# The expert's VectorE and ScalarE work put behind attention's own in each step, and weights four steps later

## The chip, the cores and the metric

The kernel runs on one core of a Trainium2 chip. The metric is the device time of one execution in microseconds, the median of several runs. [...] Each engine works through its own queue in the order in which it was given.

## The reference

Attention with a causal mask over 2 batches, 12 heads, 448 positions and a head width of 64; then two feed-forward layers over the 896 x 768 result.

```python
# attention, per batch and head
scores = scale * q @ k.T ; scores masked above the diagonal
attn   = exp(scores - max) / (sum + 1e-9)
x      = (attn @ v), heads side by side        # 896 x 768
# first layer (w_in 768 x 2048, w_out 2048 x 768)
h = x @ w_in ; g = h - tanh(h) ; x = g @ w_out
# second layer (w_a, w_b 768 x 1536, w_out 1536 x 768)
out = ((x @ w_a) * (x @ w_b)) @ w_out
```

All is in float32; the weights arrive as float64, read as pairs of 32-bit words.

## The kernel before, in words

**Precision.** A product is made of three TensorE matmuls: each operand is split into a high part of reduced precision and a low part, and `matmuls` (L189 to 196) adds high x high, high x low and low x high. So every weight tile needs preparation, and so does every activation.

**Weights.** A weight tile (768 x 128 for `w_in`) goes through five stages. `load_part` (L105) issues half of it as a transfer on SP. `magnitude` (L119) takes the absolute value of the high word on ScalarE (L125). `bits_step` (L134) does four VectorE operations, one at a call (L142, L144, L148, L152), that turn the two words of a float64 into one float32; the last one frees the raw buffer, of which there are two. `split` (L159) rounds to the high part `wh` on ScalarE (L166) and subtracts to get the low part `wl`, on POOL during attention (L168).

**Attention.** Heads go in pairs: 12 pairs `i`, each with 4 row blocks `c` of 112 queries, give 48 units. The loop in `attention` takes steps j = 0 to 51. Step j issues, in this order for every engine: the scores of unit j (L263, into two `s` banks); the transposes of unit j - 2's weights (`turn_p`, L307, into `t` banks, with every third turn in the `h` bank for the first 24 units); in steps with c = 1 and c = 2 the products with the values of the pair before (L328), and in c = 2 the transposes of the reciprocal sums (`turn_r`, L345); then on ScalarE and VectorE what was put off. `later_act` holds ScalarE's copies out of the `t` banks (L318, L354); it runs first. Then `top` (L275, VectorE, the masked minimum, which also moves the scores out of their bank) and `exps` (L287, ScalarE). Then `later_dve`: VectorE's copies (L316) and `divide` (L357, with POOL's L358 and L359, which split the result). In steps with c = 0 there follow the reciprocal of the sums (L337, VectorE, which waits for POOL's L401), its widening (L339) and the split of the next pair's `q` and `k` (L250, L251), both on POOL.

**Expert work inside attention.** `filler` is called three times a step. Its third call feeds the weights: loads in steps 3, 6, 9 and 12, and from step `WEIGHTS_AT` on one `bits` call a step, a `magnitude` where j % 4 is 0, a `split` where it is 1, and loads from step 24 on. From step 28 on the first two calls issue three and two matmuls of the first layer for the first batch. `early` makes five such tiles of 128 hidden units, each of 18 matmuls into the one `h` bank. A tile takes four steps, and the next one starts two steps after the last one's end: tiles begin in steps 28, 33, 38, 43 and 48 and end in steps 31, 36, 41, 46 and 51. A tile needs its weights split two steps earlier. `hidden` (L428) then queues the tile's element work: `tanh` (L441, ScalarE), `rest` (L437, VectorE: h - tanh, the last reader of the `h` bank), and in the step after that `gh` (L438, ScalarE) and `gl` (L439, VectorE). In the kernel before, these go into the same two queues as attention's work: `tanh` ahead of the step's `exps`, `rest` behind the step's copies and ahead of `divide`.

**Who sets the order.** Attention is written inside `manual_schedule`, so the order of its instructions on each engine is the written one. What follows, the other batch's part of the tiles and both layers, is ordered by a planner; it may put such instructions between attention's. Its matmuls go to `s`, `h`, `t` and `o` banks in a cycle, and a bank of a name is given out in the written order.

Of the kernel before, what the change touches and what calls it, by code (L numbers as in the profile page):

```python
# [48 lines left out]
def attention_moe_moe2(ctx, tc, q, k, v, w_in, w_out, w_a, w_b, w_o, out):  # L49
    nc = tc.nc  # L50
    B, H, S, D = v.shape
# [1 line left out]
    DFF1 = w_in.shape[1]  # L53
    DFF2 = w_a.shape[1]
    XLAG = 7
    WEIGHTS_AT = 16
    GROUP_P = (2, 4, 3, 4)
    QC = 112
    NQ = S // QC
# [17 lines left out]
    def bank(tag):  # L77
        return ps.tile([128, 512], F32, tag=tag, name=tag, bufs=BANKS[tag])
# [50 lines left out]
    def bits(steps):  # L129

        for _ in range(steps):
            bits_step()
# [68 lines left out]


    later_act, later_dve, turn_no = [], [], [0]
    in_attention = [True]
    xh, xl = {}, {}

    def attention(filler):
        with ExitStack() as st:
# [45 lines left out]
            def scores(j):  # L254

                i, c = units[j]
                n = (c + 1) * QC
                cs = slice(c * QC, n)
                sc[j] = [bank("s")[:QC, :n], bank("s")[:QC, :n]]
                for x, (a, b_) in enumerate(parts[i]):  # L260
                    for e in range(2):
                        r = slice(64 * e, 64 * e + 64)
                        nc.tensor.matmul(  # L263
                            sc[j][e], a[r, 0, cs], b_[r, 1, :n], start=x == 0, stop=x == len(parts[i]) - 1
                        )
# [32 lines left out]
            def turn_p(j):  # L298

                i, c = units[j]  # L300
                p = pr.pop(j).rearrange("q h (k s) -> q (h k) s", s=QC)
                nb = 2 * (c + 1)
                for a in range(0, nb, GROUP_P[c]):
                    g = GROUP_P[c]
                    pst = turn_bank(j)
                    for x in range(g):
                        nc.tensor.transpose(  # L307
                            out=pst[:QC, x * QC:(x + 1) * QC], in_=p[:, a + x], identity=ident[:QC, :QC]
                        )
                    out_ = pts[c // 2][:, :, :c + 1, c % 2]  # L310
                    if g == nb:
                        in_ = pst[:QC, :g * QC].rearrange("s (e k q) -> s e k q", e=2, q=QC)
                    else:
                        out_, in_ = out_[:, a // g], pst[:QC, :g * QC].rearrange("s (k q) -> s k q", q=QC)
                    if c in (0, 2) or (c == 3 and a):
                        later_dve.append(lambda o=out_, p=in_: nc.vector.tensor_copy(out=o, in_=p))  # L316
                    else:
                        later_act.append(lambda o=out_, p=in_: nc.scalar.copy(out=o, in_=p))  # L318

            def values(i, h):  # L320

                vt, o = vs[i % NV], bank("o") if h == 0 else ot[i]
                ot[i] = o
                for k_ in range(2 * h + 2):
                    c0 = max(2 * h, k_)
                    cs = slice(c0 * QC, (2 * h + 2) * QC)
                    for e in range(2):
                        nc.tensor.matmul(  # L328
                            o[64 * e:64 * e + 64, cs], vt[:, k_, e, :],
                            pts[h][:, e, k_, c0 - 2 * h:].rearrange("s c q -> s (c q)"),  # L330
                            start=k_ == 0, stop=k_ == 2 * h + 1, skip_group_check=True,
                        )
# [9 lines left out]
            def turn_r(i):  # L342
                r, pst, o = sums.pop(i), turn_bank(NQ * i), ot[i]
                for c in range(NQ):
                    nc.tensor.transpose(  # L345
                        out=pst[:, c * QC:(c + 1) * QC], in_=r[:, c].rearrange("q h d -> q (h d)"),
                        identity=ident[:QC, :QC],
                    )
                b, kk = pairs[i]
                if kk not in xh:  # L350
                    xh[kk], xl[kk] = [xp.tile([128, NT], F32R, tag=x, name=x) for x in ("xh", "xl")]
                hi, lo = [t[kk][:, b * S:(b + 1) * S] for t in (xh, xl)]
                x, y = [sp.tile([128, S], F32, tag=t, name=t, bufs=2) for t in "xy"]
                later_act.append(lambda: nc.scalar.copy(out=y, in_=pst[:, :S]))  # L354

                def divide():
                    nc.vector.tensor_tensor(out=x, in0=o[:, :S], in1=y, op=ALU.mult)  # L357
                    nc.gpsimd.tensor_copy(out=hi, in_=x)  # L358
                    nc.gpsimd.tensor_tensor(out=lo, in0=x, in1=hi.bitcast(F32), op=ALU.subtract)  # L359

                divides.append(lambda: later_dve.append(divide))

            def run(queue):
                todo, queue[:] = queue[:], []
                for f in todo:
                    f()
# [5 lines left out]
            for j in range(n + XLAG - 3):  # L372
                i, c = divmod(j, NQ)
                filler(j, 0)
                if j < n:
                    scores(j)
                if 0 <= j - 2 < n:
                    turn_p(j - 2)
                filler(j, 1)
                if j >= 5 and c == 1:  # L380
                    values(i - 1, 0)
                if j >= 5 and c == 2:
                    turn_r(i - 1)
                    values(i - 1, 1)
                if c == 3:
                    run(divides)
                if j < n and c == 1:
                    load(i + 2, "qk")
                if j < n and c == 2:
                    load(i + 2, "v")  # L390
                run(later_act)
                if j < n:
                    top(j)
                    exps(j)
                run(later_dve)
                if j >= 4 and c == 0:
                    weigh(i - 1)
                if j < n and c == 0:
                    split_qk(i + 1)
                if j < n and c == 3:  # L400
                    nc.gpsimd.tensor_scalar_add(out=sums[i], in0=sums[i], scalar1=1e-9)  # L401
                filler(j, 2)
            run(later_act)
            run(later_dve)
            by_hand.__exit__(None, None, None)

    cycle = ["s", "h", "s", "t", "s", "o", "s", "t"]
# [5 lines left out]
    gh, gl, gw, g_full = {}, {}, {}, []  # L413
# [14 lines left out]
    def hidden(w, cs, hi, lo, h, act, dve):  # L428

        wh, wl = w  # L430
        n = cs.stop - cs.start
        yield from matmuls(h, [((wh[:, kk], wl[:, kk]), (xh[kk][:, cs], xl[kk][:, cs])) for kk in range(KD)])
        th = ep.tile([128, 512], F32, tag="e0", name="e0")[:, :n]
        gg = ep.tile([128, 512], F32, tag="e1", name="e1")[:, :n]

        def rest():
            nc.vector.tensor_tensor(out=gg, in0=h, in1=th, op=ALU.subtract)  # L437
            act(lambda: nc.scalar.copy(out=hi, in_=gg))  # L438
            dve(lambda: nc.vector.tensor_tensor(out=lo, in0=gg, in1=hi.bitcast(F32), op=ALU.subtract))  # L439

        act(lambda: nc.scalar.activation(out=th, in_=h, func=ACTF.Tanh))  # L441
        dve(rest)

    def now(f):
        f()
# [1 line left out]
    held = []  # L447

    def early():
        for f in range(GROUPS1[0]):  # L450
            held.append(next_weights())
            new_g(f)
            yield from hidden(
                held[f], slice(0, S), gh[f, 0], gl[f, 0], bank("h")[:, :S], later_act.append, later_dve.append
            )
            yield "done"

# [9 lines left out]
    def filler(j, part):  # L467

        n0 = NPAIR * NQ
        if part == 2:  # L470
            if j in (3, 6, 9, 12):
                load_part()
            if j >= WEIGHTS_AT:
                if j % 4 == 1:
                    split()
                    while len(split_at) < at["halve"]:
                        split_at.append(j)
                bits(1)
                if j % 4 == 0:
                    magnitude()  # L480
                if j % 4 in (0, 1) and j >= n0:
                    load_part()
        if j < XLAG + n0 - 3:
            return
        for _ in range((3, 2, 0)[part]):
            if j >= rest_until[0] and (under_way[0] or (split_at + [n0] * 9)[len(held)] + 2 <= j) and step():
                rest_until[0] = j + 2

    def drain():
        while later_act or later_dve:  # L490
            todo = later_act + later_dve
            later_act.clear()
            later_dve.clear()
            for f in todo:
                f()

# [141 lines left out]
```

## Time and profile before

| | before |
|---|---|
| runs (median, lowest, highest) | 613.17, 611.48, 614.2 us |
| the profiled execution: its own time, its span | 611.09 us, 609.4 us |
| TensorE busy | 596.5 us (98%) |
| VectorE busy | 411.6 us (68%) |
| ScalarE busy | 259.2 us (43%) |
| POOL busy | 95.1 us (16%) |
| mean granted TensorE clock | 0.994 |

The span runs from the first instruction to the last; the execution's own time adds what lies around it. Busy shares are means over the whole span: POOL works during the first 142 us alone. [...] A timeline gives the start, the duration, the engine, the line, the operation, output and input, how many instructions were merged, and in brackets the idle time ahead of it and what ended it. Instructions of one engine overlap a little, so the distance from one start to the next is what an instruction costs its queue.

### The profile page before, as it was taken

To read this page: it belongs to the slowest core of one execution; us is meant where nothing else is said; L and a number is where in the kernel's file an instruction comes from. 1 tells how busy PE (TensorE), PEld (TensorE's weight loads), DVE (VectorE), ACT (ScalarE), POOL (GpSimd) and SP (SyncE) were. 2 spreads that over 40 slices of the span, in tenths; PEclk is the share of its full clock that TensorE was granted. 3 is DMA by queue.
4 is the path that set the end of the run, shared out by engine and by line. 5 is a ranking of instruction groups with operands and counts; after the bars stand their busy time and mean duration, and the time that the engine had idled before them with its cause. 6 is when DMAs were issued, how large, how long until landed. Compare 5 with 4: busy or idle time off the path is not lost.

```text
span 609.4 us, 8997 instructions
## 1 busy us (share of the span) xinstructions
PE 596.5 (98%) x3384; PEld 521.2 (86%) x3384; DVE 411.6 (68%) x771; ACT 259.2 (43%) x519; POOL 95.1 (16%) x106
## 2 busy tenths in 40 slices
PE   8998989999999999999999999999999999999997
PEld 4665666689998988888898888899999999989997
DVE  5677668957988999767889976666600789862211
ACT  5776667634555654224444443333411554331000
POOL 5689578531000000000000000000000000000000
PEclk9999989999999999999999999999999999999999
DMA  6533333114354444333333333333300335500111
GB/s 193 170 91 99 112 98 113 64 45 139 128 182 156 156 150 145 117 108 103 106 104 104 103 118 122 123 107 116 119 23 0 101 116 188 168 0 1 52 66 66
DMA packets 64971, 65.07 MB, mean 107 GB/s; under 512 B 13984, under 2 KB 61856, under 8 KB 64928
## 3 DMA queue, kind: packets, MB, share of 16 engines
q1 hardware_dynamic: 64928, 64.50, 33.5%
q8 instruction: 27, 0.44, 0.3%
q14 instruction: 16, 0.13, 0.1%
HBM read 61.73 MB, written 2.75 MB: 106 GB/s over the span
## 4 chain that ended last, share of the span: by engine, by line
PE 89%; DVE 4%; POOL 4%; issue 1%; DMA 1%; SPq 0%; ACT 0%; DVEq 0%; POOLq 0%; ACTq 0%
PE s L194 41%; PE t L194 19%; PE h L194 11%; PE o L194 10%; PE o L328 3%; PE s L263 2%; PE t L307 2%; DVE p L275 1%; POOL xl L359 1%; POOL xh L358 1%; POOL qkl L251 1%; DVE pt L316 1%; DMA qk<-in_q 1%; PE t L345 1%; DVE x L357 1%
## 5 line engine op out<-in xcount | busy, mean ns | idle before, releaser
L125 ACT ACTIVATE t<-raw 128x768 f32<-128x768 f32 (+1 forms) x70 | 62.0, 886 | 90.1 <-DMA raw<-in_moe_w_out 32.1
L168 DVE TENSOR_TENSOR wl<-t,wh 128x768 fp32r<-128x768 f32 (+1 forms) x63 | 58.6, 932 | 51.8 <-ACT wh L166 51.4
L194 PE MATMUL s<-xh,wl 128*128 128x512 f32 (+2 forms) x222 | 82.8, 373 | 0.0
L194 PE MATMUL s<-xl,wh 128*128 128x512 f32 (+2 forms) x222 | 82.6, 372 | 0.0
L194 PE MATMUL s<-xh,wh 128*128 128x512 f32 (+2 forms) x222 | 82.4, 371 | 0.0
L166 ACT CAST wh<-t 128x768 fp32r<-128x768 f32 (+1 forms) x70 | 56.8, 815 | 50.6 <-PE t L194 16.9
L148 DVE SCALAR_TENSOR_TENSOR t<-raw,t 128x768 int32<-128x768 int32 (+1 forms) x70 | 65.5, 936 | 0.9
L152 DVE SCALAR_TENSOR_TENSOR t<-raw,t 128x768 int32<-128x768 int32 (+1 forms) x70 | 64.8, 925 | 0.8
L142 DVE TENSOR_SCALAR t<-t 128x768 f32<-128x768 f32 (+1 forms) x70 | 39.6, 566 | 29.8 <-ACT t L125 29.8
L287 ACT ACTIVATE p<-p,m 112x112 f32<-112x112 f32 (+3 forms) x96 | 49.9, 522 | 16.6 <-DVE m L275 16.4
L275 DVE CUSTOM_DVE_ANT_0 p<-s,mask 112x112 f32<-112x112 f32 (+3 forms) x96 | 39.0, 444 | 23.1 <-PE s L263 22.9
L194 PEld LDWEIGHTS s<-xh,wh 128*128 128x128 f32 x222 | 41.7, 188 | 5.8 <-issue 0.3
L194 PEld LDWEIGHTS s<-xl,wh 128*128 128x128 f32 x222 | 41.7, 188 | 5.6
L194 PEld LDWEIGHTS s<-xh,wl 128*128 128x128 f32 x222 | 41.6, 188 | 5.6
L144 DVE TENSOR_SCALAR t<-t 128x768 int32<-128x768 int32 (+1 forms) x70 | 41.0, 587 | 1.1
L194 PE MATMUL t<-xh,wl 128*128 128x384 f32 (+2 forms) x114 | 40.3, 354 | 0.0
L194 PE MATMUL t<-xh,wh 128*128 128x384 f32 (+2 forms) x114 | 40.3, 354 | 0.0
L194 PE MATMUL t<-xl,wh 128*128 128x384 f32 (+2 forms) x114 | 40.3, 353 | 0.0
L307 PE MATMUL t<-ident,p 112*112 112x112 f32 x202 | 30.3, 274 | 4.3 <-DVE pt L316 4.0
L194 PE MATMUL h<-xh,wh 128*128 128x448 f32 (+2 forms) x90 | 33.7, 374 | 0.6 <-DVE e L437 0.6
L194 PE MATMUL h<-xl,wh 128*128 128x448 f32 (+2 forms) x90 | 33.0, 367 | 0.0
L194 PE MATMUL h<-xh,wl 128*128 128x448 f32 (+2 forms) x90 | 33.0, 366 | 0.0
(148 smaller groups left out, 1311.8 us busy)
## 6 DMA issues: line engine op xcount, KB each, us to landing
raw<-in_moe_w_out SPq DMA_DIRECT2D x48, 384.0 KB, 3.4
raw<-in_moe_w_in SPq DMA_DIRECT2D x32, 384.0 KB, 3.9
raw<-in_moe_w_a SPq DMA_DIRECT2D x24, 384.0 KB, 3.9
raw<-in_moe_w_b SPq DMA_DIRECT2D x24, 384.0 KB, 3.7
raw<-in_moe_w_out SPq DMA_DIRECT2D x12, 256.0 KB, 3.5
qk<-in_q SPq DMA_DIRECT2D x12, 224.0 KB, 3.5
qk<-in_k SPq DMA_DIRECT2D x12, 224.0 KB, 4.3
v<-in_v SPq DMA_DIRECT2D x24, 112.0 KB, 2.7
```

Of the source, the lines that this page charges most:

```text
L125: nc.scalar.activation(out=t.bitcast(F32), in_=raw[:, 0:nk, :, 1].bitcast(F32), func=ACTF.Abs)
L142: nc.vector.tensor_scalar(out=tf, in0=tf, scalar1=LOWEST, scalar2=HIGHEST, op0=ALU.max, op1=ALU.min)
L144: nc.vector.tensor_scalar(out=t, in0=t, scalar1=3, scalar2=0x3FFFFFF8, op0=ALU.logical_shift_left, op1=ALU.bitwise_and)
L148: nc.vector.scalar_tensor_tensor(out=t, in0=low, scalar=29, in1=t, op0=ALU.logical_shift_right, op1=ALU.bitwise_or)
L152: nc.vector.scalar_tensor_tensor(out=t, in0=high, scalar=-0x40000000, in1=t, op0=ALU.bitwise_and, op1=ALU.bitwise_or)
L166: nc.scalar.copy(out=hi[:, 0:nk], in_=t.bitcast(F32))
L168: engine.tensor_tensor(out=lo[:, 0:nk], in0=t.bitcast(F32), in1=hi[:, 0:nk].bitcast(F32), op=ALU.subtract)
L194: nc.tensor.matmul(o, a, b_, start=j == 0, stop=j == n - 1)
L275: nc.vector.tensor_tensor_reduce(out=p[:, e, :], in0=s, in1=mask[:, S - n:], scale=-scale, scalar=-MASKED, op0=ALU.add, op1=ALU.min, accum ...
L287: nc.scalar.activation(out=p[:, e, :], in_=p[:, e, :], func=ACTF.Exp, bias=m[e], scale=-1.0, accum_out=sums[i][:, c, e:e + 1],)
L307: nc.tensor.transpose(out=pst[:QC, x * QC:(x + 1) * QC], in_=p[:, a + x], identity=ident[:QC, :QC])
L328: nc.tensor.matmul(o[64 * e:64 * e + 64, cs], vt[:, k_, e, :], pts[h][:, e, k_, c0 - 2 * h:].rearrange("s c q -> s (c q)"), start=k_ == 0, ...
```

## The change

Three things change. Weight preparation begins in step 20 in place of 16, and the four early loads are issued in steps 4, 8, 12 and 16 in place of 3, 6, 9 and 12. The expert's element work gets queues of its own, `last_act` and `last_dve`, which run in each step behind `later_act`, `top`, `exps` and `later_dve`. And during attention `rest` is queued a second time when its turn comes, so it runs one step after `tanh`; `gh` and `gl` run one step after `rest`. After the last step `drain` empties all four queues.

```diff
-    WEIGHTS_AT = 16
+    WEIGHTS_AT = 20
...
+    last_act, last_dve = [], []
...
                 run(later_dve)
+                run(last_act)
+                run(last_dve)
                 if j >= 4 and c == 0:
                     weigh(i - 1)
...
-            run(later_act)
-            run(later_dve)
+            drain()
...
         act(lambda: nc.scalar.activation(out=th, in_=h, func=ACTF.Tanh))
-        dve(rest)
+        dve((lambda: dve(rest)) if in_attention else rest)
...
-                held[f], slice(0, S), gh[f, 0], gl[f, 0], bank("h")[:, :S], later_act.append, later_dve.append
+                held[f], slice(0, S), gh[f, 0], gl[f, 0], bank("h")[:, :S], last_act.append, last_dve.append
...
-            if j in (3, 6, 9, 12):
+            if j in (4, 8, 12, 16):
                 load_part()
...
     def drain():
-        while later_act or later_dve:
-            todo = later_act + later_dve
-            later_act.clear()
-            later_dve.clear()
+        queues = (later_act, later_dve, last_act, last_dve)
+        while any(queues):
+            todo = [f for q_ in queues for f in q_]
+            for q_ in queues:
+                q_.clear()
             for f in todo:
                 f()
```

## Rows read from the trace of the kernel before

**Rows 1.** Busy time by stretch: stretch, length, each engine (instructions), TensorE's clock, DMA share, GB/s.

```profile
41.00:51.00 10.00, 9.09 (x72) 6.44 (x72) 7.95 (x27) 7.34 (x21) 9.28 (x10) 0.83 0.24 67
...
73.00:88.50 15.50, 13.34 (x90) 9.10 (x88) 10.07 (x33) 9.13 (x25) 10.19 (x9) 0.89 0.34 98
...
140.00:300.00 160.00, 160.00 (x792) 144.78 (x791) 134.79 (x202) 73.26 (x116) 2.50 (x2) 1.00 0.41 134
```

**Rows 2.** Timeline of TensorE, steps 16 to 28.

```profile
32.98 0.30 PE L263 MATMUL s<-qkh 64*112 64x112 f32 x2
...
40.95 0.31 PE L263 MATMUL s<-qkh 64*112 64x112 f32 x2
42.17 0.31 PE L263 MATMUL s<-qkl,qkh 64*112 64x112 f32 x2 [0.91 <-POOL qkl L251]
...
54.57 0.57 PE L307 MATMUL t<-ident,p 112*112 112x112 f32 x4 [1.28 <-DVE pt L316]
...
57.94 0.57 PE L345 MATMUL t<-ident,wide 112*128 112x112 f32 x4 [1.10 <-DVE pt L316]
...
61.57 0.36 PE L194 MATMUL h<-xh,wl 128*128 128x448 f32 x1
61.86 0.31 PE L263 MATMUL s<-qkh 64*112 64x112 f32 x2
```

**Rows 3.** The chain that ended last: start, duration, what.

```profile
42.20 1.23 POOL xh L358
...
51.00 1.80 POOL wl L168
```

**Rows 4.** Instructions on tile `wl` to 135 us: duration min/median/max in ns.

```profile
L168 POOL TENSOR_TENSOR wl<-t,wh x7: 1556/1838/2401, 51.0 to 129.8; 128x768 fp32r<-128x768 f32 x5, 128x640 fp32r<-128x640 f32 x2
```

**Rows 5.** Timeline of TensorE, step 33.

```profile
74.93 0.47 PE L194 MATMUL h<-xh,wh 128*128 128x448 f32 x1 [0.60 <-DVE e L437]
...
77.76 1.38 PE L307 MATMUL t<-ident,p 112*112 112x112 f32 x8 [1.46 <-DVE pt L316]
```

**Rows 6.** Timeline of VectorE, steps 31 and 32.

```profile
73.47 0.08 DVE L275 DVE_READ_ACCUMULATOR2_ANT m<- 112x1 f32 x1
74.25 0.62 DVE L437 TENSOR_TENSOR e<-h,e 128x448 f32<-128x448 f32 x1 [0.69 <-ACT e L441]
74.79 0.61 DVE L357 TENSOR_TENSOR x<-o,y 128x448 f32<-128x448 f32 x1
...
76.58 0.62 DVE L439 TENSOR_TENSOR gl<-e,gh 128x448 fp32r<-128x448 f32 x1
77.11 0.91 DVE L316 COPY pt<-t 112x336 f32<-112x336 f32 x2
```

**Rows 7.** Timeline of ScalarE, steps 31 and 32.

```profile
73.67 0.55 ACT L441 ACTIVATE e<-h 128x448 f32<-128x448 f32 x1
...
75.41 0.56 ACT L438 CAST gh<-e 128x448 fp32r<-128x448 f32 x1
```

**Rows 8.** Timeline of TensorE, step 38.

```profile
92.29 0.47 PE L194 MATMUL h<-xh,wh 128*128 128x448 f32 x1
...
94.86 0.58 PE L345 MATMUL t<-ident,wide 112*128 112x112 f32 x4 [0.31 <-DVE pt L316]
```

**Rows 9.** Timeline of VectorE, step 37.

```profile
93.26 0.92 DVE L439 TENSOR_TENSOR gl<-e,gh 128x448 fp32r<-128x448 f32 x1
94.11 0.61 DVE L316 COPY pt<-t 112x448 f32<-112x448 f32 x1
```

**Rows 10.** Timeline of TensorE, steps 43 to 45.

```profile
107.47 0.47 PE L194 MATMUL h<-xh,wh 128*128 128x448 f32 x1
...
114.23 0.98 PE L307 MATMUL t<-ident,p 112*112 112x112 f32 x8 [0.86 <-DVE pt L316]
```

**Rows 11.** Timeline of VectorE, step 42.

```profile
107.52 1.35 DVE L439 TENSOR_TENSOR gl<-e,gh 128x448 fp32r<-128x448 f32 x1
108.79 0.38 DVE L316 COPY pt<-t 112x224 f32<-112x224 f32 x1
```

## The prediction

> **What bounds the kernel now.** I read the page's engine shares first: TensorE is busy for 98% of the span, so only time in which it waits or runs at half clock can move. The table by stage places that time [rows 1]: from 140 to 300 us TensorE is busy for 160 of 160 us at full clock, while 41 to 51 us has 9.09 of 10 at a granted clock of 0.83, and 73 to 88.5 us has 13.34 of 15.5 at 0.89. All of it lies in attention, which the change edits. [...]
>
> Next, TensorE's timeline gave the steps. The 64x112 score matmuls open a pair of heads, so steps 16, 20 and 28 begin at 32.98, 40.95 and (after three expert matmuls) 61.86 us [rows 2]. The waits in between are 0.91 us for POOL's `qkl`, then 1.28 and 1.10 us for VectorE's copies. The chain of waits says why VectorE is late: it runs over POOL alone from 42.20 to beyond 51.00 us, where tile 0's `wl` (1.80 us) ends at 52.80 [rows 3]. So while weights are prepared and no expert matmul stretches TensorE's steps, POOL sets the pace. From step 28 on, the waits are hand-overs between TensorE and VectorE: 0.60 us for L437 (it frees the only `h` bank) and 1.46 us for L316 [rows 5], then 0.31 us [rows 8] and 0.86 us [rows 10].
>
> **Weights at step 20, loads at 4, 8, 12, 16.** No instruction is added; the first two tiles' preparation moves by four steps. Before, tile 0 ran over steps 16 to 20 and tile 1 over 20 to 24, then nothing was ready until step 28. Now tile 0 has 20 to 24, tile 1 24 to 28, tile 2 28 to 32, and the splits fall at 25, 29, 33, 37, 41. The expert tiles still start at steps 28, 33, 38, 43, 48.
>
> Step 16 to 20 becomes free of weights; I leave it at its 7.97 us [rows 2], since it carried little before. Steps 20 to 28 then repeat what 16 to 24 did, with the same VectorE, ScalarE and POOL programs. There `wl` ended 52.80 - 32.98 = 19.82 us after step 16 began [rows 2, 3]; in the new kernel that is 40.95 + 19.82 = 60.77 us. But step 28 opens with three matmuls of expert tile 0, and the third reads `wl`. Before, it ran at 61.57, long after `wl`; now it waits for it. It starts at 60.77 and the scores of step 28 about 0.29 us later (61.57 to 61.86), at 61.06: **0.8 us saved**. Best bound: if POOL kept up, TensorE would need 40.95 + 2 x 7.97 + 0.9 for the three matmuls (3 x 0.29) = 57.8, which saves 4.1 us. Other bound: the slowest `wl` took 2.40 us, the middle one 1.84 [rows 4], so 0.6 us later, saving 0.2. I take 0.8, since the repeated program has rows for every part.
>
> The two VectorE waits (1.28 and 1.10 us) move to steps 29 and 30, which now hold eight and fifteen expert matmuls at about 0.2 us each; 1.6 and 3 us of TensorE work cover them. Without that cover they cost up to 2.4 us. SP's loads cost nothing: tile 2's load at step 24 now waits for tile 0's last bit operation and holds up the `q` and `k` loads of step 25 behind it, but those are needed three steps later. The four early loads move past loads on a queue that no TensorE wait after 33 us names.
>
> **Expert tile 0's hand-over (steps 31 to 33).** Now `tanh` runs behind the step's exponentials and L437 one step later, behind the copies. Before, VectorE was free at 73.55, waited for `tanh` until 74.25, ran L437 until the division at 74.79, ran `gl` from 76.58 to 77.11, and then the copies [rows 6]. Of those 3.56 us, 0.70 (wait), 0.54 and 0.53 move behind the copies: the copies start at 73.55 + 1.79 = 75.34, take 0.91, and L437 runs 76.25 to 76.86. `tanh` has been done by then: it now starts where the exponentials end, which with `tanh` ahead of them was at 75.41, so it ends by 75.41 + 0.55 = 75.96 [rows 7]. So the first matmul of tile 1 starts at 76.92, where it stood at 74.93; the 1.46 us wait behind it is gone, and the next transposes come 77.76 - 1.46 - 74.93 = 1.37 us later, at 78.29 instead of 77.76 [rows 5]: **0.5 us lost**. One wait has become another. Scores, transposes and values of step 33 all stand behind this waiting matmul.
>
> **Tile 1's (steps 36 to 38).** The same wait has no cover here. Before, L437 ran in step 36, and the first matmul of tile 2 started at 92.29 with no idle time [rows 8]. Now step 37 runs its scores' minimum, the copy (in `gl`'s place at 93.26; 0.53 to the next instruction [rows 9]) and then L437, from 93.79 to 94.40. TensorE arrives at 92.29 and waits until 94.46: 2.17 us. The 0.31 us wait at 94.86 goes: **1.9 us lost**. The minimum is no earlier than before: VectorE waits for POOL's `sum` ahead of it, whatever L437 does. Bounds: 2.2 lost, if nothing is given back; nothing, if VectorE reaches L437 2.2 us sooner.
>
> **Tile 2's (steps 41 to 43).** L437 leaves its place in step 41 (0.53 to the next instruction, as in [rows 6]), so the copy of 108.79, now ahead of `gl`, starts at 107.52 - 0.53 = 106.99, takes 0.30 to the next instruction, and L437 ends at 107.90; TensorE's 107.47 becomes 107.96, 0.5 later. The 0.86 us wait at 114.23 absorbs most of this, as VectorE has the same instructions to do before the copies that end it [rows 10, 11]. But `gl` now stands behind ScalarE's exponentials. It took 0.62 at tile 0 and 1.35 us here [rows 6, 11]; with 0.7 us either way the bounds are -0.5 and +0.9; I take **0.2 us lost**, nearest to no change.
>
> [...]
>
> Tiles 3 and 4 hand over after the last scores, where TensorE has the other batch's matmuls between attention's: nothing, with 0.5 us either way for another mix.
>
> **The sum:** -0.8 + 0.5 + 1.9 + 0.2 = +1.8 us. The profiled execution took 611.09 us (span 609.4), which makes 612.9; it lies 2.1 under the median of 613.17, on which the forecast stands: **615.0 us**, own range 613.4 to 616.6. No measurable change: 0.5% (3.1 us) is about what a measurement of this kernel tells from none.
>
> **Rivals.**
> *The clock falls at the new waits (slower).* Place: step 28 (`wl`) and step 38 (`h`). For: it fell after the 0.91 us wait and after 0.60 + 1.46. Against: 1.28 and 1.10 us passed at full clock [rows 1, 2, 5]. It decides if a wait of 1.3 to 2.2 us starts a fall that the next one does not hide: 1.7 us for each, so 616.7 for one and 618.4 for both. [...]
>
> *POOL keeps up (faster).* Saving 4.1 in place of 0.8, and the fall behind the 1.46 us wait gone (1.7): -4.1 + 2.6 - 1.7 = -3.2, so 610.0. For: POOL's instructions there were stretched by VectorE's. Against: VectorE's program moves along with POOL's, so the same ones meet.
>
> *The hand-overs cost nothing (faster).* The first matmul of each tile finds its bank free, and the waits of 0.60, 1.46, 0.31 and 0.86 us go with the fall behind them: -0.8 - 3.2 - 1.7 = -5.7, so 607.4. Against: L437 would have to end 2.2 us sooner in step 37.
>
> *The change does not do what it says:* the planner might put other work into the waits. Against: the first work outside the hand-written order needs an `s` bank, which comes after attention's last scores. It would give 613 us.
>
> **From cases to numbers.** Forecast 0.45, clock 0.28, POOL 0.14, free hand-overs 0.08, planner 0.05. Faster by over 0.5%: the free hand-overs and most of POOL, 0.19. Slower: most of the clock case and the forecast's upper edge, 0.31. Between: 0.50. The range, 609.5 to 618.6, reaches over POOL and both falls.
>
> **What would show it.** Right: TensorE waits for POOL's `wl` in step 28, for L437 by about 2 us in steps 33 and 38, and no longer by 1.46 us for the copies; step 28 comes about 0.8 us sooner and step 47 about 1.8 later. Wrong: no wait on `wl`, or expert tile 2 starting without a wait; a granted clock of 1.00 at 73 to 88 us would take 1.7 us off, one under 1.00 behind step 38 add it.

## The result, and the profile after

The changed kernel is slower: 619.26 us median of 4 runs (617.5 to 624.2) against 613.42; the ratio is 1.0112, with a 95% interval from 1.0076 to 1.0149. A second, longer series of the same kernel gave 618.81 (8 runs, 615.01 to 621.1) against 612.39, ratio 1.0084 (1.0049 to 1.0119). The ratios are estimated from the executions themselves, so they differ a little from the quotient of two medians. The forecast was no change, 615.0 us.

The lines of the code moved by one to three: `qkl` is L252, the scores L264, VectorE's copies L317, h - tanh L439, `gh` L440 and `gl` L441. The profiled execution took 617.51 us with a span of 615.6, 6.2 more than before.

The table by stage of the changed kernel shows where TensorE lost its clock; columns as in [rows 1], with PE for TensorE, DVE for VectorE, ACT for ScalarE, POOL for GpSimd and SP for SyncE in all lines. The clock is a share of full speed. In windows of one microsecond from 4 to 160 us every trace reads 1.00 or 0.50, and a value between only where the clock changes (in the kernel before 0.50 from 44 to 47 us, 0.79 in the next, then 1.00). "Half rate" below is the 0.50.

```profile
8.00:18.00 10.00, 7.83 (x62) 5.91 (x62) 5.36 (x21) 5.52 (x19) 6.88 (x9) 0.83 0.52 132
...
51.00:64.00 13.00, 9.50 (x86) 6.47 (x84) 11.20 (x32) 9.09 (x26) 12.19 (x12) 1.00 0.45 132
...
74.00:84.00 10.00, 7.47 (x48) 5.21 (x46) 7.80 (x22) 6.45 (x18) 7.42 (x9) 0.83 0.32 84
...
96.00:105.00 9.00, 8.54 (x51) 5.97 (x51) 4.80 (x14) 3.68 (x11) 4.66 (x4) 0.81 0.49 150
...
140.00:300.00 160.00, 160.00 (x797) 143.60 (x796) 134.87 (x200) 72.02 (x113) 3.82 (x3) 1.00 0.42 132
```

From 140 us on nothing changed: 160 of 160 us at full clock. Before, the clock was low around 44 and 78 us (0.50 from 44 to 47 and from 78.5 to 81.5); now it is around 11, 79 and 96 us (0.50 from 12 to 14, 80 to 82 and 97 to 100). The stage with the weights (51 to 64 us) runs at full clock, but TensorE stands idle for 3.5 of its 13 us, and POOL is busy for 12.19.

TensorE's timeline, the answer to [rows 2, 5, 8, 10]:

```profile
9.67 0.31 PE L264 MATMUL s<-qkh 64*112 64x112 f32 x2 [1.27 <-POOL qkh L251]
10.88 0.31 PE L264 MATMUL s<-qkl,qkh 64*112 64x112 f32 x2 [0.90 <-POOL qkl L252]
...
35.50 0.31 PE L264 MATMUL s<-qkh 64*112 64x112 f32 x2
...
63.15 0.47 PE L194 MATMUL h<-xh,wl 128*128 128x448 f32 x1 [1.61 <-POOL wl L168]
63.55 0.31 PE L264 MATMUL s<-qkh 64*112 64x112 f32 x2
...
78.45 0.47 PE L194 MATMUL h<-xh,wh 128*128 128x448 f32 x1 [2.44 <-DVE e L439]
...
90.58 0.31 PE L264 MATMUL s<-qkh 64*112 64x112 f32 x2
...
96.46 0.61 PE L194 MATMUL h<-xh,wh 128*128 128x448 f32 x1 [2.10 <-DVE e L439]
...
105.19 0.31 PE L264 MATMUL s<-qkh 64*112 64x112 f32 x2
...
120.14 0.98 PE L308 MATMUL t<-ident,p 112*112 112x112 f32 x8 [1.55 <-DVE pt L317]
```

Steps 36 and 40 in the kernel before:

```profile
88.56 0.30 PE L263 MATMUL s<-qkh 64*112 64x112 f32 x2
...
100.00 0.30 PE L263 MATMUL s<-qkh 64*112 64x112 f32 x2
```

Read the step starts off such lines (16, 28, 36, 40, 44 and 47 before: 32.98, 61.86, 88.56, 100.00, 110.63, 119.93; after: 35.50, 63.55, 90.58, 105.19, 115.86, 125.85) and the 6.2 us fall into place:

| stretch | before, us | after, us | difference | forecast |
|---|---|---|---|---|
| start to step 16 | 32.98 | 35.50 | +2.52 | 0 |
| 16 to 28 (weights) | 28.88 | 28.05 | -0.83 | -0.8 |
| 28 to 36 (tile 0's hand-over) | 26.70 | 27.03 | +0.33 | +0.5 |
| 36 to 40 (tile 1's) | 11.44 | 14.61 | +3.17 | +1.9 |
| 40 to 44 | 10.63 | 10.67 | +0.04 | +0.2 with the next |
| 44 to 47 (tile 2's) | 9.30 | 9.99 | +0.69 | |
| step 47 to the end | 489.47 | 489.75 | +0.28 | 0 |

VectorE's timeline shows the two late L439 operations and what `gl` waits for; the answer to [rows 6, 9, 11]:

```profile
77.78 0.62 DVE L439 TENSOR_TENSOR e<-h,e 128x448 f32<-128x448 f32 x1
...
82.89 1.16 DVE L441 TENSOR_TENSOR gl<-e,gh 128x448 fp32r<-128x448 f32 x1 [0.64 <-ACT gh L440]
...
95.79 0.61 DVE L439 TENSOR_TENSOR e<-h,e 128x448 f32<-128x448 f32 x1
...
102.78 0.62 DVE L441 TENSOR_TENSOR gl<-e,gh 128x448 fp32r<-128x448 f32 x1 [2.56 <-ACT gh L440]
...
117.33 1.12 DVE L441 TENSOR_TENSOR gl<-e,gh 128x448 fp32r<-128x448 f32 x1 [1.22 <-ACT gh L440]
...
119.50 0.91 DVE L317 COPY pt<-t 112x336 f32<-112x336 f32 x2
```

L439 ends at 78.40 and 96.40 and the waiting matmul starts 0.05 and 0.06 us later. The wait of 1.22 us for `gh` stands ahead of the copies at 119.50, for which TensorE waits 1.55 us; between them VectorE has `gl` itself, one operation on weights (L148) and the minima of the step (L276).

### The profile page after: what moved, and what is told of

It is laid out like the page before. It is cut to its first block, busy times and chain, and to the rows that moved or that the text cites. A ratio compares the mean times of both kernels' runs of the same rounds, so it can differ in the third digit from the quotient of the medians.

```text
span 615.6 us, 8996 instructions
## 1 busy us (share of the span) xinstructions
PE 598.0 (97%) x3384; PEld 522.2 (85%) x3384; DVE 412.8 (67%) x771; ACT 258.6 (42%) x519; POOL 93.3 (15%) x106
## 4 chain that ended last, share of the span: by engine, by line
PE 90%; DVE 3%; POOL 3%; issue 1%; DMA 1%; ACT 1%; SPq 0%; DVEq 0%; POOLq 0%; ACTq 0%
PE s L194 40%; PE t L194 19%; PE h L194 12%; PE o L194 10%; PE o L329 3%; PE s L264 3%; PE t L308 2%; DVE p L276 1%; POOL qkl L252 1%; DMA qk<-in_q 1%; POOL xl L360 1%; POOL xh L359 1%; PE h L308 1%; PE t L346 1%; DVE pt L317 1%
## 5 line engine op out<-in xcount | busy, mean ns | idle before, releaser
L148 DVE SCALAR_TENSOR_TENSOR t<-raw,t 128x768 int32<-128x768 int32 (+1 forms) x70 | 65.9, 941 | 0.9
L276 DVE CUSTOM_DVE_ANT_0 p<-s,mask 112x112 f32<-112x112 f32 (+3 forms) x96 | 39.0, 445 | 25.1 <-PE s L264 25.0
```

The costliest lines, as they stand in the source:

```text
L148: nc.vector.scalar_tensor_tensor(out=t, in0=low, scalar=29, in1=t, op0=ALU.logical_shift_right, op1=ALU.bitwise_or)
L276: nc.vector.tensor_tensor_reduce(out=p[:, e, :], in0=s, in1=mask[:, S - n:], scale=-scale, scalar=-MASKED, op0=ALU.add, op1=ALU.min, accum ...
```

## The experiments

"Half-rate time" below is worked out from the mean granted clock of an execution, with half rate at a clock of 0.50: 2 x (1 - clock) x span. In the kernel before it is 7.3 us in most executions (3.6 to 21.0 in all), in the changed one 7.4 to 27.4 us. Ratios are to the kernel before on the same chip, with 95% intervals. The chips differ a little: the kernel before has a median of 612.07 us beside e1, e2, e3 and e5, of 612.99 beside e4, e6, e7 and e8, and of 612.39 beside the rest. So compare ratios, not medians, between these groups.

| label | what differs | median, us | ratio | mean half-rate time, us |
|---|---|---|---|---|
| e1_weights | the weights part alone | 614.6 | 1.0037 (1.0013 to 1.0060) | 11.4 |
| e2_order | the order part alone | 622.69 | 1.0147 (1.0078 to 1.0217) | 21.1 |
| e3_oldloads | changed, early loads as before | 617.6 | 1.0101 (1.0059 to 1.0142) | 12.0 |
| e4_rest_same | changed, h - tanh in its own step | 612.59 | 0.9989 (0.9956 to 1.0023) | 11.0 |
| e5_mixed | before, VectorE's expert work last | 610.6 | 0.9985 (0.9969 to 1.0001) | 8.8 |
| e6_scores_first | changed, scores ahead of the waiting matmul | 612.51 | 1.0002 (0.9973 to 1.0032) | 7.8 |
| e7_dummies | changed, TensorE kept busy in two waits | 613.12 | 1.0018 (0.9995 to 1.0041) | 3.8 |
| e8_weights_dve | e1 with tile 0's `wl` on VectorE | 610.63 | 0.9973 (0.9945 to 1.0000) | 5.6 |
| after_again | the changed kernel again | 618.81 | 1.0084 (1.0049 to 1.0119) | 13.1 |
| e9_both | e5 and e8 together | 609.1 | 0.9953 (0.9932 to 0.9974) | 3.2 |
| e10_both_warm | e9 with dummies in three waits | 608.27 | 0.9928 (0.9905 to 0.9952) | 0.2 |

**The weights part alone** (e1_weights).

```diff
-    WEIGHTS_AT = 16
+    WEIGHTS_AT = 20
...
-            if j in (3, 6, 9, 12):
+            if j in (4, 8, 12, 16):
```

> The weights part alone: preparation from step 20, loads in steps 4, 8, 12 and 16, the expert's element work as in the kernel before. Theory 1 (the forecast's terms, and the 2.5 us that the new kernel lost before step 16 came from the first transfers' landing, not from the change): 0.8 us faster than before, step 28 begins about 0.8 us sooner counted from step 16, TensorE waits 1.2 to 1.7 us for POOL's wl there, step 16 begins at 33 us or, where the first q lands late, near 35. Theory 2 (moving the early loads slows the start): step 16 always begins near 35.5 and the kernel is 1.7 us slower than before.

It is 0.4% slower, not 0.8 us faster. Its timeline and its table by stage:

```profile
63.34 0.47 PE L194 MATMUL h<-xh,wl 128*128 128x448 f32 x1 [1.61 <-POOL wl L168]
```

```profile
64.00:68.00 4.00, 4.00 (x24) 3.12 (x23) 2.60 (x9) 1.65 (x5) 3.53 (x5) 0.57 0.01 4
```

Step 28 begins 28.04 us after step 16, so the 0.84 us are there again, and so is the wait on `wl`. But here the clock falls behind this wait (0.57 from 64 to 68 us), and steps 28 to 32 take 12.44 us instead of 10.94. That is 1.5 us, more than the gain. From step 36 to 47 it takes 31.37 us, exactly as before: the weights part does nothing there. Of the 3.4 us that this trace is longer than that of the kernel before, 2.73 lie ahead of step 16, which begins at 35.71 us; whether the moved loads do that is the question of e3_oldloads.

**The order part alone** (e2_order).

```diff
-    WEIGHTS_AT = 20
+    WEIGHTS_AT = 16
...
-            if j in (4, 8, 12, 16):
+            if j in (3, 6, 9, 12):
```

> The order part alone: the separate queues and the L437 operation one step later, weights from step 16 and loads in steps 3, 6, 9 and 12 as before. Theory 1: 3 to 4.5 us slower than before (0.3 at tile 0's hand-over, 2.2 of waiting at tile 1's and 1.0 more if the clock falls behind it, 0.7 at tile 2's); TensorE waits about 2 us for L437 in steps 33 and 38 each. Theory 2 (the hand-overs are given back later and the loss is the start's): within 1.5 us of before.

The order part is 1.5% slower by itself, more than expected; with four executions the interval is wide and reaches over that of the whole change. TensorE's timeline and the table by stage:

```profile
38.60 0.31 PE L264 MATMUL s<-qkh 64*112 64x112 f32 x2
...
82.28 0.47 PE L194 MATMUL h<-xh,wh 128*128 128x448 f32 x1 [2.43 <-DVE e L439]
...
100.27 0.74 PE L194 MATMUL h<-xh,wh 128*128 128x448 f32 x1 [2.11 <-DVE e L439]
```

```profile
11.00:22.00 11.00, 11.00 (x64) 7.92 (x66) 4.19 (x17) 3.97 (x14) 4.09 (x6) 0.53 0.18 55
82.00:87.00 5.00, 4.72 (x27) 3.51 (x27) 2.58 (x8) 2.35 (x7) 4.45 (x7) 0.66 0.42 136
99.00:107.00 8.00, 6.73 (x31) 4.62 (x33) 3.39 (x10) 3.72 (x11) 5.38 (x5) 0.57 0.42 141
```

The waits are 2.43 and 2.11 us, the same as in the changed kernel, and the clock falls behind both; behind the second it stays down for about 7 us (0.43 x 8 / 0.5), twice what I had priced. The first row of each fence is about the start: all work ahead of step 16 is as in the kernel before, and yet step 16 begins at 38.60 instead of 32.98, behind a clock that was down for 10 us.

**The early loads** (e3_oldloads).

```diff
-            if j in (4, 8, 12, 16):
+            if j in (3, 6, 9, 12):
```

> The changed kernel with its four early loads back in steps 3, 6, 9 and 12. Theory 1: the loads do nothing, so the same times as the changed kernel: 615 us with an undisturbed start and 617.5 with a late first landing. Theory 2: step 16 begins near 33 us always, and 2.5 us are won against the changed kernel, 615.

The ratio of 1.0101 is that of the changed kernel: the loads do nothing that can be measured. Step 16 began at 33.91 here, and the execution still took 618.41, since the clock fell three times later:

```profile
61.00:66.00 5.00, 4.45 (x24) 3.57 (x24) 3.75 (x9) 2.10 (x7) 4.22 (x5) 0.66 0.04 8
78.00:83.00 5.00, 4.63 (x25) 3.42 (x27) 2.67 (x8) 2.31 (x7) 4.45 (x7) 0.66 0.41 107
95.00:103.00 8.00, 6.64 (x31) 4.55 (x33) 3.49 (x10) 3.69 (x11) 5.49 (x6) 0.57 0.44 141
```

These are the places of the three new waits: `wl` in step 28, and the `h` bank in steps 33 and 38.

**Only VectorE's half of the order** (e5_mixed).

```diff
             yield from hidden(
-                held[f], slice(0, S), gh[f, 0], gl[f, 0], bank("h")[:, :S], last_act.append, last_dve.append
+                held[f], slice(0, S), gh[f, 0], gl[f, 0], bank("h")[:, :S], later_act.append, last_dve.append
...
-        dve((lambda: dve(rest)) if in_attention else rest)
+        dve(rest)
```

The weights are those of the kernel before; the lines are shown against the changed one.

> Weights as before; of the order part only VectorE's half: tanh and gh go with attention's own ScalarE work as before, h - tanh runs in the same step but behind the division, gl behind the next step's copies. Theory 1 (the loss comes from L437's later step and from gl waiting for ScalarE; putting VectorE's expert work last is itself a gain): the h bank comes free as before, VectorE no longer waits 0.70 us for tanh, the copies of step 32 come 1.0 us sooner, so 1.3 us faster than before, up to 3 if the clock fall behind step 33 goes as well. Theory 2 (putting expert work last is what costs): 1 to 3 us slower.

The median is 1.5 us under the one of before, with an interval that reaches 1.0001. Tile 0's hand-over:

```profile
80.49 0.47 PE L194 MATMUL h<-xh,wh 128*128 128x448 f32 x1 [0.60 <-DVE e L439]
82.26 0.98 PE L308 MATMUL t<-ident,p 112*112 112x112 f32 x8 [0.39 <-DVE pt L317]
```

The bank comes free as before (0.60 us), and the wait for the copies is 0.39 us instead of 1.46. So expert work last on VectorE is not what costs. In this trace it helps where the bank's reader stays in its step; in the median the gain is not clear of noise.

**h - tanh back in its own step** (e4_rest_same).

```diff
-        dve((lambda: dve(rest)) if in_attention else rest)
+        dve(rest)
```

> The changed kernel, but h - tanh (L439 there) runs in tanh's own step, not one later. Theory 1 (the later step is what costs): no 2 us waits for the h bank; the hand-overs are as in the kernel before, so what is left is the weights part: about 614.6 us, 4 to 5 less than the changed kernel. Theory 2 (putting ScalarE's expert work behind the exponentials is what costs, whatever the step): VectorE waits over 1 us for tanh in steps 31 and 41 and the time stays at 617 or more.

This one line returns the whole loss: 612.59 us, ratio 0.9989, 2 us better than expected. In its trace, that of the quickest of the ten executions, step 38 has no wait; in step 33 the wait is still 1.90 us:

```profile
75.59 0.47 PE L194 MATMUL h<-xh,wh 128*128 128x448 f32 x1 [1.90 <-DVE e L439]
...
90.36 0.47 PE L194 MATMUL h<-xh,wh 128*128 128x448 f32 x1
```

VectorE's timeline says why:

```profile
74.91 0.62 DVE L439 TENSOR_TENSOR e<-h,e 128x448 f32<-128x448 f32 x1 [1.46 <-ACT e L443]
```

That is theory 2's wait for `tanh`. With the clock at 1.00 behind it, steps 28 to 36 take 25.41 us, no more than the 25.46 that the changed kernel takes with its clock kept (e7_dummies), so little is won there. Step 38's hand-over gives back most: steps 36 to 40 take 10.94 us instead of 14.61. Steps 44 to 47 give back another 0.7 (9.30 instead of 9.99). The line changes all three at once, so their shares are read from this one trace alone.

**Scores ahead of the waiting matmul** (e6_scores_first).

```diff
+                first = j not in (33, 38, 43)
+                if first:
+                    filler(j, 0)
                 if j < n:
                     scores(j)
                 if 0 <= j - 2 < n:
                     turn_p(j - 2)
+                if not first:
+                    filler(j, 0)
                 filler(j, 1)
```

> The changed kernel with the first matmuls of tiles 1, 2 and 3 (steps 33, 38, 43) issued behind the step's scores and transposes instead of ahead of them. Theory 1 (TensorE's order turns the late h bank into an idle engine): the two waits shrink from 2.4 and 2.1 us to about 0.7 and 0.9, the clock falls behind them mostly go, 3 to 5 us are won against the changed kernel: 614 to 616. Theory 2 (VectorE paces these steps anyway): the waits move to the transposes and copies, within 1 us of the changed kernel.

```profile
75.37 0.98 PE L308 MATMUL t<-ident,p 112*112 112x112 f32 x8 [1.09 <-ACT p L288]
...
91.28 0.47 PE L194 MATMUL h<-xh,wh 128*128 128x448 f32 x1 [1.12 <-DVE e L443]
```

2.4 and 2.1 us become 1.1 and 1.1, and the time is that of the kernel before, 1.0002. Some of the wait moved to the exponentials, as theory 2 had it, and about half of it was idle time that other TensorE work could fill. In this trace no fall follows: the clock is at 1.00 from 58 us on.

**TensorE kept busy in the waits** (e7_dummies).

```diff
+                if j in (33, 38):
+                    spare[j] = [bank("s"), bank("s")]
+                    for _ in range(10):
+                        nc.tensor.matmul(spare[j][0], idle[:, 0:128], idle, start=True, stop=True)
                 filler(j, 0)
```

`scores` then takes its two banks from `spare`.

> The changed kernel with ten dummy matmuls of 512 columns (0.22 us each, into a bank that the step's scores overwrite) ahead of the waiting matmul in steps 33 and 38: TensorE works through the wait, the wait itself stays. Theory 1 (a part of the loss is the clock that falls behind these waits): granted clock 1.00 from 78 to 106 us, 1 to 3 us won against the changed kernel, about 616.5, and less spread between runs. Theory 2 (the falls come from elsewhere or cost nothing): the same 619.

```profile
76.87 0.47 PE L194 MATMUL h<-xh,wh 128*128 128x448 f32 x1 [0.27 <-DVE e L445]
```

```profile
60.00:74.00 14.00, 12.34 (x98) 8.76 (x99) 9.74 (x29) 7.62 (x23) 11.21 (x10) 1.00 0.41 124
74.00:90.00 16.00, 15.30 (x113) 10.34 (x115) 13.14 (x36) 10.48 (x32) 11.80 (x11) 1.00 0.31 94
90.00:106.00 16.00, 15.74 (x120) 10.70 (x120) 11.93 (x36) 9.98 (x28) 11.57 (x14) 1.00 0.30 86
```

The matmul waits as long as before, now behind dummies (it starts 3.53 us after the transposes ahead of it, here and in the changed kernel), and the clock stays at 1.00. No useful instruction was moved, and the ratio is 1.0018, against 1.0084 and 1.0112 in the two series of the changed kernel. In five of ten executions the half-rate time is 0.0, and those take 611.5 to 612.6 us. So more than half of the changed kernel's loss goes with the clock and not with the waiting; how much is worked out below.

**The weights part with tile 0's `wl` on VectorE** (e8_weights_dve).

```diff
-        engine = nc.gpsimd if in_attention else nc.vector
+        engine = nc.gpsimd if in_attention and i else nc.vector
```

> The weights part alone, with tile 0's wl on VectorE instead of POOL. Theory 1 (the weights part loses because tile 0's wl stands at the end of POOL's chain when step 28 asks for it, 1.6 us, and the clock falls behind that wait, 1.5 us): no wait on wl, step 28 begins 1.6 us sooner counted from step 16, no fall behind it: 611 to 612 us. Theory 2 (the weights part loses by preparing three tiles without a pause): 614 to 615 as with wl on POOL.

```profile
57.73 1.32 DVE L168 TENSOR_TENSOR wl<-t,wh 128x768 fp32r<-128x768 f32 x1 [1.04 <-ACT wh L166]
```

```profile
65.53 0.98 PE L307 MATMUL t<-ident,p 112*112 112x112 f32 x8 [0.83 <-DVE pt L316]
```

The time is a little better than expected, 610.63, 0.27% under before with an interval that reaches 1.0000, but it came about otherwise. There is no wait on `wl`, and step 28 begins 26.58 us after step 16 (61.18 - 34.60), 1.46 sooner than in e1_weights. But VectorE, which waited 1.04 us for `wh`, is late, and steps 28 to 32 take 12.61 us at full clock: the 1.5 us are given back. What stays won is the clock: half-rate time 5.6 us instead of 11.4 (7.9 and 9.4 in the kernel before on the two chips). Step 33 has the two waits of the kernel before, and here no fall behind them:

```profile
75.92 0.47 PE L194 MATMUL h<-xh,wh 128*128 128x448 f32 x1 [0.60 <-DVE e L437]
...
78.75 0.98 PE L307 MATMUL t<-ident,p 112*112 112x112 f32 x8 [1.46 <-DVE pt L316]
```

Steps 32 to 36 take 14.24 us at a clock of 1.00, where the kernel before took 15.76 (72.80 to 88.56) with its fall.

**The changed kernel again** (after_again).

> The changed kernel itself, more often. Theory 1 (its waits add about 3 us at full clock, and the clock falls that they start add as much again, more in some executions than in others): the times go with the mean granted clock, about 611 us plus half of the time spent at half rate, which lies between 10 and 27 us against 7 to 10 in the kernel before; median 617 to 620. Theory 2 (the spread has another source): no relation between the two.

Times and half-rate times of the eight executions, in us: 615.01 (7.4), 615.54 (7.4), 615.57 (7.4), 618.15 (13.6), 619.47 (13.6), 619.86 (17.3), 620.6 (21.0), 621.1 (17.3). They go together, with a slope of 0.44, near the one half that theory 1 gave. At equal half-rate time (7.3 to 7.4 us) the changed kernel takes 615.0 to 615.6 and the one before 610.7 to 613.6.

**Both gains together** (e9_both: e5's order, with the weights of e8), and **with dummies in its waits** (e10_both_warm; the diff is against e9_both, and `scores` takes its banks from `spare` as in e7).

```diff
                 i, c = divmod(j, NQ)
+                if j in (4, 24, 33):
+                    spare[j] = [bank("s"), bank("s")]
+                    for _ in range(4):
+                        nc.tensor.matmul(spare[j][0], idle[:, 0:128], idle, start=True, stop=True)
                 filler(j, 0)
```

> The two parts that gained, together: weights from step 20 with tile 0's wl on VectorE, and VectorE's expert work last in its step while ScalarE's stays in front. Theory 1 (they act in different steps, 24 to 28 and 31 to 37): the gains add up, 1.5 + 2.4 us faster than before, about 609. Theory 2 (both remove the same clock fall, or VectorE has no room for both): no better than 610.5.

> The same with four dummy matmuls (0.22 us each) ahead of the scores of steps 4, 24 and 33, where TensorE waited 0.6 to 1.4 us in every trace. Theory 1 (these waits are where the clock falls start): half-rate time near 0, another 2 to 3 us won, about 606.5. Theory 2 (the dummies only fill time or come in the way): as without them, or 0.5 us slower.

e9_both is 0.47% faster than the kernel before, e10_both_warm 0.72%, and both intervals lie clear of one. The sum held (609.1 against 609 expected), though neither part's gain was clear of noise by itself. With the dummies the clock stays up through attention:

```profile
4.00:40.00 36.00, 35.72 (x312) 24.01 (x310) 23.79 (x100) 25.52 (x88) 24.13 (x34) 1.00 0.54 158
40.00:75.00 35.00, 32.28 (x265) 21.96 (x261) 28.26 (x85) 23.63 (x69) 26.93 (x28) 1.00 0.40 113
75.00:120.00 45.00, 43.14 (x340) 31.42 (x340) 38.20 (x112) 31.04 (x88) 35.29 (x33) 1.00 0.30 93
```

They won 0.8 us by the medians, not 2 to 3: the executions of e9_both without half-rate time already take 607.6 to 608.7. What the dummies take away is the slow ones; all six executions lie between 607.5 and 608.4.

**`gh` in front on ScalarE** (e11_gh_front), one execution.

```diff
-            act(lambda: nc.scalar.copy(out=hi, in_=gg))
+            (later_act.append if in_attention else act)(lambda: nc.scalar.copy(out=hi, in_=gg))
```

> The changed kernel with gh in front of the exponentials on ScalarE, as before the change. Theory 1 (gl's waits for ScalarE, 0.64, 2.56 and 1.22 us in the changed kernel, delay the copies of step 44): VectorE no longer waits there and the 1.55 us wait in step 45 shrinks to about 0.8; the L439 waits of 2.4 and 2.1 us stay. Theory 2 (the wait in step 45 comes from L439's place): it stays at 1.5.

```profile
118.77 0.61 DVE L441 TENSOR_TENSOR gl<-e,gh 128x448 fp32r<-128x448 f32 x1
```

`gl` waits for nothing, and the wait in step 45 is not 0.8 but gone: steps 44 to 47 take 8.56 us instead of 9.99. The two L439 waits stay:

```profile
79.75 0.47 PE L194 MATMUL h<-xh,wh 128*128 128x448 f32 x1 [2.44 <-DVE e L439]
...
97.69 0.74 PE L194 MATMUL h<-xh,wh 128*128 128x448 f32 x1 [2.11 <-DVE e L439]
```

The execution as a whole took 619.30, with 17.3 us at half rate; one execution can't show a gain or a loss.

## Why the prediction was wrong

The waits came where the forecast put them, and its sum holds where the clock plays no part. The step that failed is that this sum has no term for the clock: it keeps the half-rate time of the kernel before. More half-rate time was left to a rival, "*The clock falls at the new waits (slower)*", with a chance of 0.28 and a price of 1.7 us a fall, two at most (the 1.7 us are what [rows 1] give: 10 x (1 - 0.83), and 15.5 x (1 - 0.89)). That case came true, and it was priced too low: about 4 of the 6 us of loss go with the clock, as worked out under "How much is which".

**Weights.** -0.8 forecast, -0.83 and -0.84 measured between steps 16 and 28, with the wait on `wl` where it was expected (1.61 us). What failed is that it stays a gain: in e1_weights and e3_oldloads the clock falls behind that wait, and steps 28 to 32 take 1.5 and 1.4 us more. That `wl` is the cause of the wait, e8_weights_dve shows. The prediction's eight and fifteen expert matmuls "in steps 29 and 30" are counts since step 28, as each step holds five; its conclusion held, steps 28 to 32 took 10.93 us against 10.94 and VectorE's copies kept nothing waiting there. That POOL's instructions were longer beside VectorE's work on weights shows in the kernel before: POOL's L358 took 0.56 us at 34.45 and 62.72, and 1.21 and 1.29 us at 42.20 and 52.74, where VectorE's L148 had begun just ahead of it.

**Tile 0's hand-over.** +0.5 forecast, +0.33 measured. The 1.46 us wait turned into one of 2.44 us for L439, as worked out. In this trace the clock falls behind it (0.50 from 80 to 82 us) as it did before.

**Tile 1's.** The 2.17 us wait was 2.10. The term was still short, +3.17 against +1.9, by the clock that fell at 96 us, where before there was none. Steps 36 to 40 take 13.12 us in e7_dummies, with the wait and without the fall: the wait alone is +1.7, and the fall adds 1.5. In e2_order and e3_oldloads the clock stays down twice as long, and these steps take 16.02 and 15.99 us, so there it adds 2.9. e4_rest_same takes this wait away and returns the loss; e6_scores_first and e7_dummies do so with L439 as late as before, the first by filling part of the wait with useful work, the second by keeping the clock.

**Tile 2's.** +0.2 forecast, +0.7 measured, inside the bounds but mis-sized. The 0.5 us wait for the bank did not come; L439 ends at 112.64, when TensorE is only just through with its values. The whole of the 0.7 is `gl` behind ScalarE's exponentials, as the trace of e11_gh_front shows. I had named this wait and bounded it by `gl`'s own duration, where its length is set by when ScalarE ends.

**The start.** 2.52 us of the profiled difference lie ahead of step 16, for which the forecast has no term. The first `q` for POOL landed a microsecond later (POOL's first split began at 7.34 us instead of 6.35), TensorE waited 1.27 and 0.90 us and began step 4 0.83 us later (9.67 against 8.84), and the clock fell (0.50 from 12 to 14 us): steps 4 to 16 took 25.83 us instead of 24.14. The change is not needed for it: step 16 begins at 32.98, 33.91, 38.60 and 38.66 us in four traces with the early loads of the kernel before (before, e3_oldloads, e2_order, e5_mixed), and between 33.15 and 37.99 in those with the new loads (32.94 in e10_both_warm, with its dummies). It differs from one execution to the next, in both kernels. Whether it is worse more often with the new loads, these few traces can't say.

**How much is which.** In the two series, twelve executions of the changed kernel spend 14 us at half rate on average, those of the kernel before about 9. Half of the difference is 2.7 us. The other 3 to 4 of the 6 us are waiting at full clock and a fall near 44 us that cost the kernel before nothing, since POOL set the pace there: steps 20 to 28 took 20.91 us with it, and 20.81 and 20.80 without it (e2_order, e5_mixed). So the 3.4 us of that fall count among the 9 without having cost anything, which adds 1.7 to the clock's share: about 4 us. What the waits cost by themselves, e7_dummies shows, whose clock stays at 1.00: steps 16 to 47 take 87.28 us, against 86.95 in the kernel before, of which 1.5 are the fall of step 33 (15.76 against 14.24, see e8_weights_dve). That makes about 2 us, near the forecast's 1.8. The forecast's 615.0 is also what the changed kernel takes in its three quickest executions of the second series, those with the half-rate time that the kernel before mostly has; that it fits so well is partly luck, as the kernel before is at 612.39 on that chip and the sum would give 614.2.

`gl` took 0.62 us at 102.78, where POOL stood idle, and 1.16 and 1.12 us at 82.89 and 117.33, each behind a POOL subtraction that had begun before it (at 82.44 and 116.82). That is half a microsecond each; it did not decide here.

The clock is what decided: in the changed kernel's trace the waits of 2.44 and 2.10 us had half rate behind them (0.50 from 80 to 82 and from 97 to 100 us). The 1.61 us wait of the same trace had none (1.00 from 63 to 74 us). No run shows what decides whether a fall follows a wait.

## What to carry to other kernels

When an operation moves later, look first at whether it is the last reader of a buffer with a single copy: everything behind the next writer waits for it, here 2.44 and 2.10 us, however idle the engine was that it made room on. Price a new TensorE wait of a microsecond or two with the clock fall behind it (here 1.4 to 2.9 us at steps 28 and 38), and fill it: useful work ahead of the waiting matmul (ratio 1.0002), or else dummies (1.0018), returned the loss here with the late reader left in place. And compare executions by their time at half rate as well as by their medians; one profile is one draw.

## What the runs showed of the hardware that was not expected

The same wait does not always have the same sequel. The 1.6 us wait on `wl` passed at full clock in the changed kernel's first trace (1.00 from 63 to 74 us) and was followed by half rate in e1_weights (0.57 over 4 us). The waits of 0.60 and 1.46 us in step 33 had a fall behind them in the kernel before (0.50 from 78.5 to 81.5 us) and none in e8_weights_dve (1.00 through steps 32 to 36). Behind the 2.1 us wait in step 38 half rate lasted about 3.5 us in one trace (0.81 over 9 us) and about 7 in two others (0.57 over 8 us). At the start it lasted over 10 us in one (0.53 over 11 us, in e2_order), with TensorE busy for all of the 11.

A fall cost nothing where POOL set the pace. Half rate near 44 us changed steps 20 to 28 by 0.1 us (20.91 with it, 20.81 and 20.80 without), while a fall in steps 32 to 36 cost 1.5 us (15.76 against 14.24).

The clock column does not show that the first matmuls are slow. It reads 1.00 from 0 to 5 us in the traces of the kernel before and of the changed one, where the first eight 128x512 matmuls (from 1.25 us on) take 3.59 and 3.47 us. In e10_both_warm, whose mean clock over the whole span is 1.00, they take 3.60 us, and four of the same shape at 8.64 us take 1.03. So a half-rate time of 0.0 leaves the start out.
